# Transposing x0 by batch tile instead of by feature tile, in a six-layer cross network

## The chip, the core and the metric

The kernel runs on one core of a Trainium2 chip, which is trn2. The metric is the device time of one execution in microseconds (us). The time before is the median of six runs.

Engines carry these names in the profile: PE is TensorE's matmul, PEld its weight load, DVE is VectorE, ACT is ScalarE, POOL is GpSimd, SP is SyncE, which here only issues transfers. A name such as L466 is line 466 of the kernel before.

## What is computed

```python
B, F, D, L = 1024, 26, 32, 6
Din = min(F * D, 1024)          # 832
# x0 (1024, 832), ws (6, 832, 832), bs (6, 832), all bfloat16

def reference(x0, ws, bs):
    x = x0
    for l in range(ws.shape[0]):
        x = x0 * (x @ ws[l] + bs[l]) + x
    return x
```

## The kernel before

The kernel keeps x transposed: features on the 128 partitions, the batch of 1,024 along the free dimension. 832 features are six whole tiles of 128 (`KFULL` = 6) and a rest of 64 (`REM`). The rest tile is folded: partitions 0 to 63 hold its first 512 batch rows, partitions 64 to 127 the other 512. So there are `KT` = 7 feature tiles and `BT` = 8 batch tiles of 128 rows (`HBT` = 4 is half of them). The order of all work is written out by hand, engine by engine, with semaphores; no scheduler moves anything.

**The stage in front.** x0 lies in HBM with the batch along the rows. SP loads it into `x0_nat` with three transfers by columns (`x0_dma`, L278): feature tiles 0 and 1, tiles 2 and 3, tiles 4 to 6. GpSimd builds the identity matrix `ident` and then issues the load of the biases, `b_raw` (L348). TensorE first runs `N_WARM` = 24 matmuls on `ident` alone (L364), whose result nobody reads. Then it goes through the feature tiles: tile `kt` takes eight transposes (L397), one for each batch tile, into a PSUM bank of its own in `tr_bank`; the rest tile takes two groups of four (L405, L412). Before feature tile 2 it turns the biases with eight small matmuls into `ps_x` (L371, L378), which waits for `sem_bias`. DVE copies feature tiles 0 to 5 to SBUF, into `x0T`, one copy of 128 x 1024 each (L552); ACT copies `bias_T` (L496) and the rest tile (L504). TensorE begins the layers when all seven copies are done:

```python
eng.wait_ge(sem_cp_v, n_cp_v)
eng.wait_ge(sem_cp_a, n_cp_a)
```

**The layers.** For each layer and each of its seven output tiles (a column group of the weights), TensorE runs seven feature tiles times two batch halves, 14 matmuls with 512 moving columns (L466), into one of two pairs of PSUM banks, `ps_y0` to `ps_y3`. ACT adds the bias on the way to SBUF (L517), DVE multiplies by x0 (L562) and adds x (L576). The last layer's tiles are transposed back and stored.

**The weights.** Layer 0's come in three parts: two blocks of 128 output columns on SP (`w0_dma_block`, L241 to L248) behind x0, and the other 576 columns on ACT's queue (`w0_dma_rest`, L256 to L263), issued once the second x0 transfer has landed. The first matmul of an output tile in layer 0 waits for the part that it needs. Layers 1 to 5 are loaded on SP (L218 to L231), each issued when the layer before it has finished its first item.

Of the kernel before, what the change touches and what calls it, by code (L numbers as in the profile page):

```python
# [5 lines left out]
ACT_F = mybir.ActivationFunctionType  # L6
ALU = mybir.AluOpType
BF16 = mybir.dt.bfloat16
# [3 lines left out]
def bass_standalone__dcn_v2_cross__recsys_kernel(  # L12
# [6 lines left out]
    B, D = x0.shape  # L19
    L = ws.shape[0]  # L20
    P = 128
    NW = 512
    assert B == 2 * NW and D % P == 64 and B % P == 0
    BT = B // P
    HBT = BT // 2
    NCH = 2
    KFULL = D // P
    KT = KFULL + 1
    REM = D - KFULL * P
    RB = KFULL * P  # L30
    NB_COLS = L * KT
# [55 lines left out]
    with ExitStack() as es:  # L87
# [7 lines left out]
        def new_sem(name):  # L95
            return es.enter_context(nc.semaphore(name))

        ident = sb("ident", [P, P], BF16)
# [15 lines left out]
        ps_t1 = psm("ps_t1", [P, 1024], BF16)  # L114
        ps_b = psm("ps_b", [P, NW], FP32)
        ps_x = psm("ps_x", [P, NW], FP32)
        x0_groups = [(0, 2), (2, 4), (4, KT)]
        sem_x0 = [new_sem(f"sem_x0_{i}") for i in range(len(x0_groups))]
        sem_bias = new_sem("sem_bias")
        sem_w = [new_sem(f"sem_w{l}") for l in range(L)]  # L120
        sem_pool = new_sem("sem_pool")
# [20 lines left out]
        ps_t = [ps_t0, ps_t1]  # L142
        xT_bufs = [xT_a, xT_b]

        tr_bank = [
            ps_t0[:, :],
            ps_t1[:, :],
            ps_y0[:, :].bitcast(BF16),
            ps_y1[:, :].bitcast(BF16),
            ps_y2[:, :].bitcast(BF16),  # L150
            ps_y3[:, :].bitcast(BF16),
            ps_b[:, :].bitcast(BF16),
        ]
        assert len(tr_bank) >= KT
        cp_on_act = [False] * KT
        cp_on_act[KT - 1] = True
        cp_wait = []
        n_cp_v = 0
        n_cp_a = 0
        for kt in range(KT):  # L160
            if cp_on_act[kt]:
                n_cp_a += 1
                cp_wait.append((True, n_cp_a))
            else:
                n_cp_v += 1
                cp_wait.append((False, n_cp_v))

        assert NPE == 2
        s_last = (NG - 1) % 2
# [102 lines left out]
        x0_v = x0.rearrange("(bt p) d -> p bt d", p=P)  # L272

        def x0_dma(eng, gi):
            k0, k1 = x0_groups[gi]
            c0 = k0 * P
            c1 = min(k1 * P, D)
            eng.dma_start(x0_nat[:, :, c0:c1], x0_v[:, :, c0:c1]).then_inc(sem_x0[gi], 16)  # L278

        xfin = None  # L280

# [27 lines left out]

        @block.sync  # L310
        def _(eng):
            x0_dma(eng, 0)
            x0_dma(eng, 1)
            x0_dma(eng, 2)
            for jb in range(W0_NBLK):
                w0_dma_block(eng, jb)
            for l in range(1, L):
                eng.wait_ge(sem_mm, mm_items_done_before_layer_start(l))
                w_dma_a(eng, l)
                w_dma_b(eng, l)  # L320
                w_dma_r(eng, l)
            for k in range(len(out_groups)):
                eng.wait_ge(sem_dve, out_groups[k][1] + 1)
                out_transpose(eng, k)
            for (k, c) in pe_pieces:
                if c != 1:
                    continue
                if piece_on_act[(k, c)]:
                    eng.wait_ge(sem_ocpa, piece_wait[(k, c)])
                else:  # L330
                    eng.wait_ge(sem_ocp, piece_wait[(k, c)])
            final_store(eng, 1, sem_out2)
            eng.wait_ge(sem_out2, 16)

        @block.gpsimd
        def _(eng):
            eng.memset(ident[:], 0.0).then_inc(sem_pool, 1)
            eng.wait_ge(sem_pool, 1)
            eng.affine_select(  # L339
                out=ident[:],  # L340
                in_=ident[:],
                compare_op=ALU.not_equal,
                fill=1.0,
                base=0,
                pattern=[[-1, P]],
                channel_multiplier=1,
            ).then_inc(sem_pool, 1)
            eng.dma_start(b_raw[0:L, :], bs[:, :]).then_inc(sem_bias, 16)  # L348
            for k in range(len(out_groups)):
                eng.wait_ge(sem_tro[k], out_transpose_count(k))  # L350
                out_store(eng, k)
            eng.wait_ge(sem_out, 16 * len(out_groups))

        SEM_POOL_WARM = 2
        N_WARM = 24
        ALT_KT_ORDER = False
        BIAS_TR_AFTER_KT = 1
        assert BIAS_TR_AFTER_KT + 1 < KT

        @block.tensor  # L360
        def _(eng):
# [23 lines left out]
                    if last:  # L385
                        mm.then_inc(sem_bt, 1)

            for kt in range(KT):
                pt = tr_bank[kt]
                if kt == BIAS_TR_AFTER_KT + 1:  # L390
                    bias_transposes()
                for gi, (k0, k1) in enumerate(x0_groups):
                    if kt == k0:
                        eng.wait_ge(sem_x0[gi], 16)
                if kt < KFULL:
                    for bt in range(BT):
                        eng.matmul(  # L397
                            pt[:, bt * P : (bt + 1) * P],
                            lhsT=x0_nat[:, bt, kt * P : (kt + 1) * P],
                            rhs=ident[:, :],  # L400
                            is_transpose=True,
                        ).then_inc(sem_tr, 1)
                else:
                    for bt in range(HBT, BT):
                        eng.matmul(  # L405
                            pt[:, (bt - HBT) * P : (bt - HBT + 1) * P],
                            lhsT=x0_nat[:, bt, D - P : D],
                            rhs=ident[:, :],
                            is_transpose=True,
                        ).then_inc(sem_tr, 1)  # L410
                    for bt in range(HBT):
                        eng.matmul(  # L412
                            pt[0:REM, bt * P : (bt + 1) * P],
                            lhsT=x0_nat[:, bt, RB:D],
                            rhs=ident[:, :],
                            is_transpose=True,
                        ).then_inc(sem_tr, 1)
            eng.wait_ge(sem_cp_v, n_cp_v)
            eng.wait_ge(sem_cp_a, n_cp_a)
            for g, (l, j) in enumerate(groups):  # L420
# [69 lines left out]

        @block.scalar
        def _(eng):
            eng.wait_ge(sem_x0[1], 16)
            w0_dma_rest(eng)
            eng.wait_ge(sem_bt, 1)
            eng.activation(bias_T[:, 0:NB_COLS], ps_x[:, 0:NB_COLS], ACT_F.Copy).then_inc(  # L496
                sem_bc, 1
            )
            for kt in range(KT):
                if not cp_on_act[kt]:  # L500
                    continue
                eng.wait_ge(sem_tr, BT * (kt + 1))
                ncol = B if kt < KFULL else NW
                eng.activation(x0T[:, kt, 0:ncol], tr_bank[kt][:, 0:ncol], ACT_F.Copy).then_inc(  # L504
                    sem_cp_a, 1
                )
            eng.wait_ge(sem_bc, 1)
            for f in range(NF - 1):
                l, j, c = items[f]
                g = group_pos[(l, j)]  # L510
                s = g % 2
                slot = f % TB_R
                if f >= TB_R:
                    eng.wait_ge(sem_dve, f - TB_R + 1)
                eng.wait_ge(sem_mm, f + 1)  # L515
                src = ps_y[s][c][:, :] if j < KFULL else ps_y[s][0][:, :]
                eng.activation(  # L517
                    t_buf[:, slot, :],
                    src,
                    ACT_F.Identity,  # L520
                    bias=bias_col(l, j),
                    scale=1.0,
                ).then_inc(sem_act, 1)
            for i, (k, c) in enumerate(pe_pieces):
                if not piece_on_act[(k, c)]:
                    continue
                j = pe_groups[k][0]
                pt = piece_psum(k, c)
                eng.wait_ge(sem_otr, HBT * (i + 1))
                eng.activation(  # L530
                    o_sb[:, c * HBT : (c + 1) * HBT, j * P : (j + 1) * P],
                    pt.rearrange("p (a b) -> p a b", b=P),
                    ACT_F.Copy,
                ).then_inc(sem_ocpa, 1)
            for (k, c) in pe_pieces:
                if c != 0:
                    continue
                if piece_on_act[(k, c)]:
                    eng.wait_ge(sem_ocpa, piece_wait[(k, c)])
                else:  # L540
                    eng.wait_ge(sem_ocp, piece_wait[(k, c)])
            final_store(eng, 0, sem_out3)
            eng.wait_ge(sem_out3, 16)

        @block.vector
        def _(eng):
            for kt in range(KT):
                if cp_on_act[kt]:
                    continue
                eng.wait_ge(sem_tr, BT * (kt + 1))  # L550
                ncol = B if kt < KFULL else NW
                eng.tensor_copy(x0T[:, kt, 0:ncol], tr_bank[kt][:, 0:ncol]).then_inc(sem_cp_v, 1)  # L552

            def emit_mult(f):
                l, j, c = items[f]
# [107 lines left out]
```

## Time and profile before

| | before |
|---|---|
| median of six runs (lowest, highest) | 139.6 us (139.29, 139.91) |
| the profiled execution's own time | 139.72 us |
| its span, first to last instruction | 137.9 us |
| TensorE busy | 127.8 us, 93% of the span |
| DVE, ACT busy | 61.8 us, 52.1 us |
| first matmul of layer 0 (L466) starts | 10.84 us |
| warm-up matmuls (L364) | 24, from 1.52 us, 2.74 us together |
| x0 transfers, issue to landing | 4.2, 5.2 and 6.6 us, issued from 0.74 to 1.87 us |
| bias transfer, issue to landing | 4.8 us, issued at 1.73 us |

Times in rows of the profile are counted from the start of the span. A row of a group gives its line, engine, operation, output and input tiles and shapes, how many there are, and what ended the idle time in front of it. The profiled execution is one execution; the part of its time outside the span, 1.8 us, belongs to no row. Matmuls are pipelined, so that a duration of one is longer than the distance from one to the next.

### The profile page before, as it was taken

To read this page: it belongs to the slowest core of one execution; us is meant where nothing else is said; L and a number is where in the kernel's file an instruction comes from. 1 tells how busy PE (TensorE), PEld (TensorE's weight loads), DVE (VectorE), ACT (ScalarE), POOL (GpSimd) and SP (SyncE) were. 2 spreads that over 40 slices of the span, in tenths; PEclk is the share of its full clock that TensorE was granted. 3 is DMA by queue.
4 is the path that set the end of the run, shared out by engine and by line. 5 is a ranking of instruction groups with operands and counts; after the bars stand their busy time and mean duration, and the time that the engine had idled before them with its cause. 6 is when DMAs were issued, how large, how long until landed. Compare 5 with 4: busy or idle time off the path is not lost.

```text
span 137.9 us, 1868 instructions
## 1 busy us (share of the span) xinstructions
PE 127.8 (93%) x692; PEld 53.9 (39%) x692; DVE 61.8 (45%) x164; ACT 52.1 (38%) x82; POOL 5.8 (4%) x12
## 2 busy tenths in 40 slices
PE   5688999999999999999999999999999999999930
PEld 5463444434344333333443334433444334433410
DVE  0370344554455544554473444463445552554570
ACT  0041444443443353333453334423444333333440
POOL 3000000000000000000000000000000000031520
PEclk9999999999999999999999999999999999999995
DMA  3996670000840001910002900005700000256757
GB/s 79 348 330 177 180 253 0 0 0 0 263 175 0 2 0 16 348 70 5 0 0 66 362 5 0 5 0 158 274 0 0 0 7 0 38 114 152 177 142 214
DMA packets 17016, 13.65 MB, mean 99 GB/s; under 512 B 7242, under 2 KB 16720, under 8 KB 17008
## 3 DMA queue, kind: packets, MB, share of 16 engines
q1 hardware_dynamic: 15136, 11.06, 27.1%
q0 software_dynamic: 400, 1.19, 3.0%
q10 hardware_dynamic: 1472, 1.29, 2.9%
q8 instruction: 5, 0.08, 0.3%
q14 instruction: 3, 0.02, 0.0%
HBM read 10.66 MB, written 1.70 MB: 90 GB/s over the span
## 4 chain that ended last, share of the span: by engine, by line
PE 84%; DMA 8%; DVE 2%; ACT 1%; issue 1%; SPq 1%; POOL 1%; DVEq 0%; ACTq 0%
PE ps_y L466 84%; DMA x_nat<-in_x_dram 5%; DMA o_sb<-xT_b 3%; ACT t_buf L517 1%; DVE x0T L552 1%; SPq L278 1%; DVE u_buf L562 1%; POOL out_dram L305 1%; PE ps_y L397 0%; DVE xT_a L576 0%; DVE xT_b L576 0%; DVEq L561 0%; ACTq L515 0%
## 5 line engine op out<-in xcount | busy, mean ns | idle before, releaser
L517 ACT ACTIVATE t_buf<-ps_y,bias_T 128x512 bf16<-128x512 f32 x77 | 49.1, 683 | 71.7 <-PE ps_y L466 71.7
L562 DVE TENSOR_TENSOR u_buf<-t_buf,x0T 128x512 bf16<-128x512 bf16 x76 | 32.1, 423 | 64.7 <-ACT t_buf L517 64.7
L466 PE MATMUL ps_y<-xT_a,w_sb 128*128 128x512 bf16 (+3 forms) x294 | 60.2, 382 | 0.3 <-DVE xT_a L576 0.3
L466 PE MATMUL ps_y<-xT_b,w_sb 128*128 128x512 bf16 (+3 forms) x196 | 39.9, 381 | 0.0
L466 PEld LDWEIGHTS ps_y<-xT_a,w_sb 128*128 128x128 bf16 (+3 forms) x294 | 23.6, 99 | 36.7 <-issue 13.2
L466 PEld LDWEIGHTS ps_y<-xT_b,w_sb 128*128 128x128 bf16 (+3 forms) x196 | 15.7, 99 | 24.1 <-issue 9.1
L466 PE MATMUL ps_y<-x0T,w_sb 128*128 128x512 bf16 (+3 forms) x98 | 19.9, 381 | 0.7 <-DVE x0T L552 0.7
L576 DVE TENSOR_TENSOR xT_b<-u_buf,xT_a 128x512 bf16<-128x512 bf16 x37 | 15.2, 419 | 0.0
L466 PEld LDWEIGHTS ps_y<-x0T,w_sb 128*128 128x128 bf16 (+3 forms) x98 | 7.8, 98 | 12.7 <-issue 4.1
L576 DVE TENSOR_TENSOR xT_a<-u_buf,xT_b 128x512 bf16<-128x512 bf16 x26 | 10.7, 420 | 0.0
L305 POOL DMA_DIRECT2D out_dram<-o_sb x5 | 4.5, 893 | 127.7 <-DMA o_sb<-xT_b 127.7
L576 DVE TENSOR_TENSOR xT_a<-u_buf,x0T 128x512 bf16<-128x512 bf16 x13 | 5.4, 420 | 0.0
L496 ACT ACT_TABLE_LOAD x1 | 1.3, 1283 | 8.3 <-issue 8.3
L364 PE MATMUL ps_x<-ident 128*128 128x128 bf16 x24 | 2.7, 313 | 1.5 <-POOL ident L339 1.5
L552 DVE COPY x0T<-ps_t 128x1024 bf16<-128x1024 bf16 x2 | 1.3, 688 | 5.6 <-PE ps_t L397 5.6
L364 PEld LDWEIGHTS ps_x<-ident 128*128 128x128 bf16 x24 | 2.5, 147 | 1.5 <-POOL ident L339 1.5
L552 DVE COPY x0T<-ps_y 128x1024 bf16<-128x1024 bf16 x4 | 2.6, 686 | 0.9 <-PE ps_y L397 0.9
L397 PE MATMUL ps_y<-ident,x_nat 128*128 128x128 bf16 x32 | 2.1, 220 | 0.4 <-DMA x_nat<-in_x_dram 0.4
L397 PEld LDWEIGHTS ps_y<-ident,x_nat 128*128 128x128 bf16 x32 | 1.8, 98 | 0.6 <-DMA x_nat<-in_x_dram 0.6
L484 PE MATMUL ps_t<-ident,xT_b 128*128 128x128 bf16 x8 | 0.8, 222 | 1.3 <-DVE xT_b L610 0.9
L397 PE MATMUL ps_t<-ident,x_nat 128*128 128x128 bf16 x16 | 1.1, 220 | 0.7 <-DMA x_nat<-in_x_dram 0.7
L397 PEld LDWEIGHTS ps_t<-ident,x_nat 128*128 128x128 bf16 x16 | 0.9, 98 | 1.0 <-DMA x_nat<-in_x_dram 1.0
(26 smaller groups left out, 10.2 us busy)
## 6 DMA issues: line engine op xcount, KB each, us to landing
w_sb<-in_ws_dram SPq DMA_DIRECT2D x10, 624.0 KB, 4.7
w_sb<-in_ws_dram SPq DMA_DIRECT2D x10, 104.0 KB, 5.2
x_nat<-in_x_dram SPq DMA_DIRECT2D x2, 512.0 KB, 4.7
out_dram<-o_sb POOLq DMA_DIRECT2D x4, 256.0 KB, 3.8
w_sb<-in_ws_dram ACTq DMA_DIRECT2D x1, 864.0 KB, 5.3
x_nat<-in_x_dram SPq DMA_DIRECT2D x1, 640.0 KB, 6.6
w_sb<-in_ws_dram SPq DMA_DIRECT2D x2, 192.0 KB, 5.6
out_dram<-o_sb SPq DMA_DIRECT2D x1, 256.0 KB, 2.3
```

The source lines that it names most:

```text
L278: eng.dma_start(x0_nat[:, :, c0:c1], x0_v[:, :, c0:c1]).then_inc(sem_x0[gi], 16)
L305: eng.dma_start(out[:, c0:c1].rearrange("(bo bi) f -> bi bo f", bi=P), o_sb[:, :, c0:c1],).then_inc(sem_out, 16)
L364: eng.matmul(ps_x[:, 0:P], lhsT=ident[:, :], rhs=ident[:, :], start=True, stop=True)
L397: eng.matmul(pt[:, bt * P : (bt + 1) * P], lhsT=x0_nat[:, bt, kt * P : (kt + 1) * P], rhs=ident[:, :], is_transpose=True,).then_inc(sem_tr, 1)
L466: mm = eng.matmul(o_ap, lhsT=lhsT, rhs=rhs, start=(kt == kt_first), stop=(kt == kt_last), tile_position=(trow, tcol), skip_group_check=(tc ...
L484: eng.matmul(pt[:, bb * P : (bb + 1) * P], lhsT=xf[:, j, bt * P : (bt + 1) * P], rhs=ident[:, :], is_transpose=True,).then_inc(sem_otr, 1)
L496: eng.activation(bias_T[:, 0:NB_COLS], ps_x[:, 0:NB_COLS], ACT_F.Copy).then_inc(sem_bc, 1)
L517: eng.activation(t_buf[:, slot, :], src, ACT_F.Identity, bias=bias_col(l, j), scale=1.0,).then_inc(sem_act, 1)
L552: eng.tensor_copy(x0T[:, kt, 0:ncol], tr_bank[kt][:, 0:ncol]).then_inc(sem_cp_v, 1)
L562: eng.tensor_tensor(u_buf[:, us, :], t_buf[:, slot, :], x0T[rows, tile, cols], ALU.mult,).then_inc(sem_u, 1)
L576: eng.tensor_tensor(xout[rows, tile, cols], u_buf[:, us, :], xin[rows, tile, cols], ALU.add,).then_inc(sem_dve, 1)
```

## The change

x0 is loaded and transposed by batch tile. Four transfers on SP bring two batch tiles each, whole rows of 832 features. TensorE goes through the eight batch tiles; each takes seven transposes into one PSUM bank, and four banks (`ps_y0` to `ps_y3`) are used in turn, so that batch tile 4 waits for the copies of batch tile 0, and so on. Each batch tile is copied with two instructions, one for its six whole feature tiles and one for the rest; even batch tiles go to DVE, odd ones to ACT. The bias transfer moves from GpSimd's queue to SP, behind the four x0 transfers; the bias matmuls stand after batch tile 3, and the ACT copy of `bias_T` between batch tiles 3 and 5. The rest of layer 0's weights moves from ACT's queue to SP, behind the two blocks. The warm-up matmuls go from 24 to 16. The layers and the output are untouched.

```diff
-        x0_groups = [(0, 2), (2, 4), (4, KT)]
+        X0_RG = 2
+        n_x0_dma = BT // X0_RG
...
-        tr_bank = [
-            ps_t0[:, :],
-            ps_t1[:, :],
+        tr_banks = [
             ps_y0[:, :].bitcast(BF16),
             ps_y1[:, :].bitcast(BF16),
             ps_y2[:, :].bitcast(BF16),
             ps_y3[:, :].bitcast(BF16),
-            ps_b[:, :].bitcast(BF16),
         ]
-        cp_on_act = [False] * KT
-        cp_on_act[KT - 1] = True
...
+        def cp_on_act_bt(bt):
+            return bt % 2 == 1
...
+        def emit_x0T_copies(eng, bt, sem):
+            bank = tr_bank_of(bt)
+            cols = slice(bt * P, (bt + 1) * P)
+            eng.wait_ge(sem_tr, KT * (bt + 1))
...
+            cp(
+                x0T[:, 0:KFULL, cols],
+                bank[:, 0 : KFULL * P].rearrange("p (a b) -> p a b", b=P),
+            )
+            c = bt // HBT
+            rows = slice(c * REM, (c + 1) * REM)
+            lcols = slice((bt - c * HBT) * P, (bt - c * HBT + 1) * P)
+            cp(x0T[rows, KFULL, lcols], bank[rows, KFULL * P : (KFULL + 1) * P]).then_inc(sem, 1)
...
         def x0_dma(eng, gi):
-            k0, k1 = x0_groups[gi]
-            c0 = k0 * P
-            c1 = min(k1 * P, D)
-            eng.dma_start(x0_nat[:, :, c0:c1], x0_v[:, :, c0:c1]).then_inc(sem_x0[gi], 16)
+            b0, b1 = gi * X0_RG, (gi + 1) * X0_RG
+            eng.dma_start(x0_nat[:, b0:b1, :], x0_v[:, b0:b1, :]).then_inc(sem_x0[gi], 16)
...
         @block.sync
         def _(eng):
-            x0_dma(eng, 0)
-            x0_dma(eng, 1)
-            x0_dma(eng, 2)
+            for gi in range(n_x0_dma):
+                x0_dma(eng, gi)
+            eng.dma_start(b_raw[0:L, :], bs[:, :]).then_inc(sem_bias, 16)
             for jb in range(W0_NBLK):
                 w0_dma_block(eng, jb)
+            w0_dma_rest(eng)
...
-            eng.dma_start(b_raw[0:L, :], bs[:, :]).then_inc(sem_bias, 16)
...
-        N_WARM = 24
+        N_WARM = 16
-        BIAS_TR_AFTER_KT = 1
+        BIAS_TR_AFTER_BT = 3
...
+            for bt in range(BT):
+                bank = tr_bank_of(bt)
+                if bt == BIAS_TR_AFTER_BT + 1:
+                    bias_transposes()
+                if bt % X0_RG == 0:
+                    eng.wait_ge(sem_x0[bt // X0_RG], 16)
+                if bt >= NBK:
+                    pb = bt - NBK
+                    eng.wait_ge(sem_cp_a if cp_on_act_bt(pb) else sem_cp_v, cp_count(pb))
+                for kt in range(KFULL):
+                    eng.matmul(
+                        bank[:, kt * P : (kt + 1) * P],
+                        lhsT=x0_nat[:, bt, kt * P : (kt + 1) * P],
+                        rhs=ident[:, :],
+                        is_transpose=True,
+                    ).then_inc(sem_tr, 1)
...
         @block.scalar
         def _(eng):
-            eng.wait_ge(sem_x0[1], 16)
-            w0_dma_rest(eng)
...
+            for bt in range(BT):
+                if cp_on_act_bt(bt):
+                    emit_x0T_copies(eng, bt, sem_cp_a)
+                if bt == BIAS_TR_AFTER_BT + 1:
+                    eng.wait_ge(sem_bt, 1)
+                    eng.activation(
+                        bias_T[:, 0:NB_COLS], ps_x[:, 0:NB_COLS], ACT_F.Copy
+                    ).then_inc(sem_bc, 1)
...
         @block.vector
         def _(eng):
-            for kt in range(KT):
-                if cp_on_act[kt]:
-                    continue
-                eng.wait_ge(sem_tr, BT * (kt + 1))
-                ncol = B if kt < KFULL else NW
-                eng.tensor_copy(x0T[:, kt, 0:ncol], tr_bank[kt][:, 0:ncol]).then_inc(sem_cp_v, 1)
+            for bt in range(BT):
+                if not cp_on_act_bt(bt):
+                    emit_x0T_copies(eng, bt, sem_cp_v)
```

More of the change, by code (lines that the diff above doesn't have):

```diff
@@ L116, in bass_standalone__dcn_v2_cross__recsys_kernel @@
         ps_x = psm("ps_x", [P, NW], FP32)
-        x0_groups = [(0, 2), (2, 4), (4, KT)]
-        sem_x0 = [new_sem(f"sem_x0_{i}") for i in range(len(x0_groups))]
+        X0_RG = 2
+        assert BT % X0_RG == 0
+        n_x0_dma = BT // X0_RG
+        sem_x0 = [new_sem(f"sem_x0_{i}") for i in range(n_x0_dma)]
         sem_bias = new_sem("sem_bias")
@@ L151, in bass_standalone__dcn_v2_cross__recsys_kernel, with tr_bank_of, cp_count @@
             ps_y3[:, :].bitcast(BF16),
-            ps_b[:, :].bitcast(BF16),
         ]
-        assert len(tr_bank) >= KT
-        cp_on_act = [False] * KT
-        cp_on_act[KT - 1] = True
-        cp_wait = []
-        n_cp_v = 0
-        n_cp_a = 0
-        for kt in range(KT):
-            if cp_on_act[kt]:
-                n_cp_a += 1
-                cp_wait.append((True, n_cp_a))
-            else:
-                n_cp_v += 1
-                cp_wait.append((False, n_cp_v))
+        NBK = len(tr_banks)
+        def tr_bank_of(bt):
+            return tr_banks[bt % NBK]
+        def cp_on_act_bt(bt):
+            return bt % 2 == 1
+        def cp_count(bt):
+            return bt // 2 + 1
+        n_cp_v = (BT + 1) // 2
+        n_cp_a = BT // 2
+        def emit_x0T_copies(eng, bt, sem):
+            bank = tr_bank_of(bt)
+            cols = slice(bt * P, (bt + 1) * P)
+            eng.wait_ge(sem_tr, KT * (bt + 1))
+            if eng is nc.vector:
+                cp = lambda o, i: eng.tensor_copy(o, i)
+            else:
+                cp = lambda o, i: eng.activation(o, i, ACT_F.Copy)
+            cp(
[6 more added lines that the diff above has]
+            cp(x0T[rows, KFULL, lcols], bank[rows, KFULL * P : (KFULL + 1) * P]).then_inc(sem, 1)
         assert NPE == 2
@@ L354, in bass_standalone__dcn_v2_cross__recsys_kernel @@
         SEM_POOL_WARM = 2
-        N_WARM = 24
+        N_WARM = 16
         ALT_KT_ORDER = False
-        BIAS_TR_AFTER_KT = 1
-        assert BIAS_TR_AFTER_KT + 1 < KT
+        BIAS_TR_AFTER_BT = 3
+        assert BIAS_TR_AFTER_BT + 1 < BT
         @block.tensor
@@ L386, in bias_transposes @@
                         mm.then_inc(sem_bt, 1)
-            for kt in range(KT):
-                pt = tr_bank[kt]
-                if kt == BIAS_TR_AFTER_KT + 1:
+            for bt in range(BT):
+                bank = tr_bank_of(bt)
+                if bt == BIAS_TR_AFTER_BT + 1:
                     bias_transposes()
[L392 to L402, printed above, removed]
-                else:
[L404 to L417, printed above, removed]
@@ new lines, in _ @@
+                if bt < HBT:
+                    eng.matmul(
+                        bank[0:REM, KFULL * P : (KFULL + 1) * P],
+                        lhsT=x0_nat[:, bt, RB:D],
+                        rhs=ident[:, :],
+                        is_transpose=True,
+                    ).then_inc(sem_tr, 1)
+                else:
+                    eng.matmul(
+                        bank[:, KFULL * P : (KFULL + 1) * P],
+                        lhsT=x0_nat[:, bt, D - P : D],
+                        rhs=ident[:, :],
+                        is_transpose=True,
+                    ).then_inc(sem_tr, 1)
@@ L492, in _ @@
         def _(eng):
-            eng.wait_ge(sem_x0[1], 16)
-            w0_dma_rest(eng)
[L495 to L500, printed above, removed]
-                    continue
-                eng.wait_ge(sem_tr, BT * (kt + 1))
-                ncol = B if kt < KFULL else NW
-                eng.activation(x0T[:, kt, 0:ncol], tr_bank[kt][:, 0:ncol], ACT_F.Copy).then_inc(
-                    sem_cp_a, 1
-                )
+            for bt in range(BT):
[6 more added lines that the diff above has]
+                    ).then_inc(sem_bc, 1)
             eng.wait_ge(sem_bc, 1)
@@ L546, in _ @@
         def _(eng):
[L547 to L552, printed above, removed]
+            for bt in range(BT):
+                if not cp_on_act_bt(bt):
+                    emit_x0T_copies(eng, bt, sem_cp_v)
             def emit_mult(f):
```

## The prediction

> **What bounds the kernel now.** I read the chain of waits first, because it says which stage decides the end.
>
> ```profile
> PE 84%; DMA 8%; DVE 2%; ACT 1%; issue 1%; SPq 1%; POOL 1%; DVEq 0%; ACTq 0%
> ...
> 1.87 6.57 DMA x_nat<-in_x_dram
> ...
> 8.48 0.63 PE ps_y L397 x8
> ...
> 9.14 1.30 DVE x0T L552 x2
> ...
> 10.84 99.37 PE ps_y L466 x490
> ```
>
> The first line is the page's share by engine, the others are pieces of the chain in order of time (start, length). From 10.84 us on TensorE runs the layers' matmuls almost without a break to the end, and the change edits nothing there. What it edits lies in front: x0 must arrive, be transposed and be copied to SBUF. So the question is one number: when does the first L466 matmul start? Each microsecond there is one of the span.
>
> Next the timeline of that stage, for ScalarE and TensorE (start, length, group, wait before it).
>
> ```profile
> 1.52 2.74 PE L364 MATMUL ps_x<-ident 128*128 128x128 bf16 x24 [1.52 <-POOL ident L339]
> ...
> 4.96 1.07 PE L397 MATMUL ps_t<-ident,x_nat 128*128 128x128 bf16 x16 [0.70 <-DMA x_nat<-in_x_dram]
> ...
> 6.62 0.42 PE L371 MATMUL ps_x<-ident,b_raw 6*128 6x6 bf16 x7 [0.59 <-DMA b_raw<-in_bs_dram]
> ...
> 6.97 1.07 PE L397 MATMUL ps_y<-ident,x_nat 128*128 128x128 bf16 x16
> ...
> 8.48 1.07 PE L397 MATMUL ps_y<-ident,x_nat 128*128 128x128 bf16 x16 [0.44 <-DMA x_nat<-in_x_dram]
> ...
> 9.58 0.21 ACT L496 ACTIVATE bias_T<-ps_x 128x42 f32<-128x42 f32 x1
> ...
> 10.15 0.60 ACT L504 ACTIVATE x0T<-ps_b 128x512 bf16<-128x512 bf16 x1 [0.36 <-PE ps_b L412]
> ```
>
> The last x0 transfer lets TensorE go at 8.48. The chain then names DVE copies ending at 10.44 and 0.41 us of "issue"; but ScalarE's copy ends at 10.15 + 0.60 = 10.75, and the matmul follows 0.09 us later. So it is ScalarE that releases the matmuls, 2.36 us after the last x0 landing.
>
> Third, the stretches after a weight load of 1,664-byte rows, issued at 13.94 on an empty queue (the last three columns: granted clock, DMA share, GB/s).
>
> ```profile
> 13.94:15.00 1.06, 1.06 (x6) 0.47 (x6) 0.27 (x1) 0.99 (x2) 0.00 (x0) 1.00 0.02 3
> 15.00:16.00 1.00, 1.00 (x6) 0.43 (x5) 0.85 (x3) 0.28 (x1) 0.00 (x0) 1.00 0.86 178
> 16.00:17.00 1.00, 1.00 (x6) 0.31 (x5) 0.07 (x1) 0.03 (x1) 0.00 (x0) 1.00 0.99 349
> 17.00:18.00 1.00, 1.00 (x6) 0.43 (x5) 0.31 (x1) 1.00 (x2) 0.00 (x0) 1.00 1.05 401
> 18.00:19.00 1.00, 1.00 (x6) 0.45 (x5) 1.00 (x4) 0.23 (x1) 0.00 (x0) 1.00 1.04 399
> ```
>
> This is the nearest row to the new x0 loads, whose rows are 1,664 bytes too: 530 KB in the first 3.06 us after the issue, then 400 GB/s. The old x0 load in 512-byte pieces runs at 345 to 350 GB/s in the same view between 4 and 7 us.
>
> **x0's arrival.** x0 is 1,704 KB. By the weight row it is through at 0.74 + 3.06 + (1,704 - 530)/400 = 6.74 us; at the old load's pace it would be about 7.6, where the old one's sum of bytes stands. I take 6.74, because piece size is what the change alters, and keep 7.6. From the last byte to TensorE's start the views give 0.67 (first weight transfer: 639 KB reached at 17.27, landed at 13.94 + 4.0), 0.79 (first x0 group: 524 KB at 4.17, start 4.96) and 0.86 (last x0 group: 7.62 to 8.48). I take 0.86, the same role, and keep 0.67. The last pair of batch tiles is then usable at 7.60, 0.88 earlier than now.
>
> **The moved bias load.** This is the step that gives the gain back. b_raw leaves GpSimd's queue, where it landed at 1.73 + 4.8 = 6.53, and stands on SP behind all four x0 transfers. TensorE waits for it after batch tile 3, and behind that wait are queued the 28 transposes of batch tiles 4 to 7, then every matmul. Tiles 4 and 5 come in the third transfer, whose 1,278 KB are through at 0.74 + 3.06 + 748/400 = 5.67, usable at 6.53; but b_raw's six rows come after the fourth. One row at 400/16 GB/s is 0.07 us, so the wait ends at 7.60 + 0.07 = 7.67 (bounds: 7.41 with the short landing, 8.5 with the old pace). Early x0 tiles thus stop paying: half the transposes start only when everything has landed.
>
> **Transposes after it.** The bias matmuls hold TensorE 6.97 - 6.62 = 0.35. Sixteen transposes take 1.07 and one 0.22, so they start (1.07 - 0.22)/15 = 0.057 apart. Tiles 4 and 5 (14 transposes) are done after 13 x 0.057 + 0.22 = 0.96; the hand-off to a copy is 0.04 (eight transposes end at 5.58, DVE starts at 5.62). ScalarE can start tile 5 at 7.67 + 0.35 + 0.96 + 0.04 = 9.02. Waits for the bank of the tile four before cost nothing: tiles 0 to 3 land by 5.5 (852 KB at 4.61, plus 0.86), their copies end by about 8, and bank reuse by tile 7 comes after 8.8. If that cover failed, each copy late would shift the end by its lateness.
>
> **Copies.** Removed: six DVE copies of 0.69 and one ACT copy of 0.60. Added per batch tile: one copy of 768 columns and one of 128. ScalarE's rows are 207 ns for 42 columns and 597 for 512, so 0.83 ns a column: 0.81 and 0.28 us. Two of ScalarE's copies in a row (L530, 595 ns each) take 1.08 together, so each follow-up gains 0.11. Tiles 5 and 7 are then 0.81 + 0.28 + 0.81 + 0.28 - 0.33 = 1.85 us (2.18 without the overlap). Tile 7's transposes are done at 9.82, before ScalarE is through with tile 5 at about 9.9, so ScalarE is busy without a gap: 9.02 + 1.85 + 0.09 = **10.96** for the first matmul. DVE's share is lighter: 422 ns for 512 and 688 for 1,024 columns give 0.55 + 0.22 a tile; tile 6, transposed by 9.4, is copied by 10.2. The bias copy of 0.21 on ScalarE falls at about 8.2, in a gap.
>
> **What costs nothing.** The ACT table load (1.28) now heads ScalarE's queue without a wait before it, and runs while x0 is on its way; if it came at the first copy instead, tile 1 would be done at about 7.6, still early. The first weight block (229 KB; 267 GB/s from 8 to 9 us) is through 0.86 after x0 and usable at about 8.5, far from 10.96. The rest of layer 0's weights moves from ScalarE's queue to SP, behind eleven other issues, which take 0.4 to 1.7 us each in the rows of before; 1,032 KB at 400 after the second block end near 12, and they are needed two column groups (6.0 us) after the first matmul, at 17. SP is free again well before layer 1's loads.
>
> **Sum.** 10.96 - 10.84 = +0.12 us. The profiled execution took 139.72 (span 137.9 and 1.8 around it); it becomes 139.84. It lies 0.12 above the median of 139.6, so the median comes to **139.7**. With the bounds (arrival 6.74 to 7.6, landing 0.67 to 0.86, no overlap on ScalarE) the first matmul lies between 10.7 and 12.1, so this case spans 139.4 to 140.9, most of it 139.4 to 140.3. A measurement here tells about 0.2% (0.28 us) from no change.
>
> **The clock.** Warm-up matmuls fall from 24 to 16. They start (2.74 - 0.31)/23 = 0.106 apart, the later transposes 0.057: TensorE doubled its pace between 4.26 and 4.96. Sixteen of them last 1.9 us, to 3.4; the transposes of tiles 0 and 1 begin near 4.3. At the end of the run, the stretch from 131.06 to 134.47 with 1.04 us of TensorE work was followed by a granted clock of 0.50; the one from 4.76 to 8.18 with 2.48 us, nearly all transposes, kept full pace.
>
> ```profile
> 4.76:8.18 3.42, 2.48 (x40) 2.10 (x40) 1.84 (x3) 0.00 (x0) 0.00 (x0) 1.00 1.16 340
> 131.06:134.47 3.41, 1.04 (x13) 0.52 (x10) 2.54 (x6) 1.45 (x3) 0.78 (x1) 1.00 0.58 141
> 134.47:137.90 3.43, 0.00 (x0) 0.00 (x0) 0.00 (x0) 0.00 (x0) 0.10 (x1) 0.50 0.74 214
> ```
>
> I read from it that transposes count as work for the clock, and that the changed kernel, with about 1.6 to 2.1 us in such a stretch, keeps it. The Trainium skill ("TensorE: Matmul & The Clock Gate", Part 4) says otherwise: transposes do not count as busy. By that rule the sum would be that of the slower rival below; the row above speaks against it, though eight small bias matmuls in that stretch keep it from being proof.
>
> **Rival, slower: the clock stays at half.** One mechanism, in TensorE, from 3.4 us on: too little work, so that the transposes behind the bias wait run 0.106 apart. It decides if the needed work in a stretch lies above some 1.6 us (the trace brackets it between 1.04 and 2.48). Tile 7 is then transposed at 7.67 + 0.35 + 27 x 0.106 + 0.31 + 0.04 = 11.23, copied 0.98 later, first matmul 12.30: +1.46. If the first layer also runs at half pace for as long as the warm-up did (at most 4.96 - 1.52 = 3.44 us), it loses half of that, 1.7: together +3.2. That is 141.1 to 142.8, and less if the clock rises midway.
>
> **Rival, faster: b_raw is not last.** If its few rows land before the fourth x0 transfer, the pipeline works as drawn. Bias and tiles 4 and 5 start at 6.53; ScalarE starts tile 5 at 6.53 + 1.35 = 7.88 and has done it at about 8.75; tile 7 is usable for TensorE at 7.60, transposed by 8.60; ScalarE ends at 9.73, first matmul 9.82: -1.02, or 138.6. Landing 0.3 before the fourth is worth about a third of it, 139.3. Against it: the x0 groups landed in the order of issue, 1.5 us or more apart. For it: the Trainium skill ("DMA: Bandwidth & Descriptors", on why a DMA increments its semaphore by 16) says a transfer of six rows runs on six engines alone, so it need not wait for the slowest of sixteen; no run here shows it.
>
> **Chances.** Main case 0.50 (of it 0.05 faster, 0.28 within 0.2%, 0.17 slower: its upper bounds reach further than its lower ones). Clock rival 0.30 (0.28 slower, 0.02 within, where the clock rises soon). Early b_raw 0.20 (0.17 faster, 0.03 within). Sums: 0.22, 0.33, 0.45. The range 139.0 to 141.2 takes the main case nearly whole, the half-early b_raw and the mild clock case; about 0.08 lies below and 0.12 above.
>
> **What would show it.** Right: the bias matmuls start within 0.2 us after the fourth x0 landing, at about 7.7, with TensorE idle for over 1 us before them; ScalarE copies tiles 5 and 7 back to back and its end, not DVE's, is followed by the first L466 matmul at about 11.0; transposes 0.057 apart; from there to the end the span keeps its 127.1 us. Wrong: bias matmuls before 7 us (early b_raw), transposes or first matmuls 0.1 or 0.4 apart (clock), a fourth x0 landing after 8 us (no gain from longer rows), or a wait for weights at the first matmul.

## The result and the profile after

| | before | after |
|---|---|---|
| median | 139.99 us (20 runs, 139.29 to 141.12) | 143.28 us (10 runs, 141.49 to 145.44) |
| the profiled execution's own time | 139.72 us | 142.53 us |
| its span | 137.9 us | 140.8 us |
| first matmul of layer 0 starts | 10.84 us | 13.70 us |

The changed kernel is slower: the ratio is 1.017, with a 95% interval of 1.0122 to 1.0217. Ratios and intervals leave out executions more than 1.5% above the fastest of the same kernel, here four of the ten after, while the medians count all; the medians alone would give 1.0235. The forecast of 139.7 us and its range, up to 141.2, both missed. In the profiled execution all of the difference lies in front of the layers: the first layer matmul moved by 2.86 us, the span by 2.9. That execution is 0.75 us below the median of its kernel; no trace of a longer one was kept.

The chain of waits after (start, length, what; the first line is the page's share by engine):

```profile
PE 84%; DMA 7%; DVE 2%; issue 2%; SPq 1%; ACT 1%; POOL 1%; DVEq 0%; ACTq 0%
...
2.77 6.17 DMA b_raw<-in_bs_dram
...
8.98 0.45 PE ps_x L385 x7
...
13.70 99.37 PE ps_y L480 x490
```

Where x0's last transfer stood in the chain, the bias load now stands: 10 KB that land 6.17 us after their issue, at 8.93. The layers' matmuls behind it take the same 99.37 us as before.

The timeline of that stage after:

```profile
1.52 1.89 PE L378 MATMUL ps_x<-ident 128*128 128x128 bf16 x16 [1.52 <-POOL ident L354]
...
3.84 0.82 PE L412 MATMUL ps_y<-ident,x_nat 128*128 128x128 bf16 x6 [0.44 <-DMA x_nat<-in_x_dram]
...
8.98 0.45 PE L385 MATMUL ps_x<-ident,b_raw 6*128 6x6 bf16 x7 [1.07 <-DMA b_raw<-in_bs_dram]
...
9.37 0.82 PE L412 MATMUL ps_y<-ident,x_nat 128*128 128x128 bf16 x6
...
11.08 1.09 ACT L174 ACTIVATE x0T<-ps_y 128x768 bf16<-128x768 bf16 x2 [1.39 <-PE ps_y L426]
...
12.22 0.25 PE L426 MATMUL ps_y<-ident,x_nat 128*128 128x128 bf16 x1
...
12.51 1.09 ACT L174 ACTIVATE x0T<-ps_y 128x768 bf16<-128x768 bf16 x2 [0.34 <-PE ps_y L426]
...
13.70 3.61 PE L480 MATMUL ps_y<-x0T,w_sb 128*128 128x512 bf16 x16 [1.23 <-issue]
```

Six transposes take 0.82 us, of which one is 0.31: they start 0.10 apart, at half pace, where before they started 0.057 apart. That holds for the first batch tile and for those after the bias wait. Only the very last one (0.25 us) is shorter, and the layers then run at full pace (16 matmuls in 3.61 us). ScalarE's copy of tile 7 begins 0.34 us after tile 5's is done: it waits for TensorE. Its end at 13.60 comes 0.10 us before the first layer matmul.

The trace also holds records of the clock that TensorE was granted. The first one of the changed kernel sets in at 12.27 us, when the last transpose was under way; this is what "the clock was raised" means below. The views print 1.00 as the clock for all time before the first record, so that half pace in front of it shows only in the distances between matmuls. Records of one trace lie whole multiples of 3.41 us apart, and the stretches below are counted back from a record in these steps (busy time and matmuls, clock, DMA share, GB/s):

```profile
2.03:5.44 3.41, 2.97 (x26) 1.00 0.97 322
5.44:8.86 3.42, 2.47 (x18) 1.00 1.01 282
8.86:12.27 3.41, 3.29 (x36) 1.00 0.71 192
```

In the experiments below the trace sometimes lacks a layer's first matmul or two. So its start is taken from ScalarE's first copy in layer 0, which begins 3.17 us later at full pace (14.01 - 10.84 before, 16.87 - 13.70 after).

### The profile page after: what moved, and what is told of

Read it like the earlier page. It is cut to its first block, busy times and chain, and to the rows that moved or that the text cites. A ratio compares the mean times of both kernels' runs of the same rounds, so it can differ in the third digit from the quotient of the medians.

```text
span 140.8 us, 1864 instructions
## 1 busy us (share of the span) xinstructions
PE 130.4 (93%) x684; PEld 55.6 (40%) x684; DVE 60.8 (43%) x166; ACT 55.6 (40%) x89; POOL 5.3 (4%) x11
## 4 chain that ended last, share of the span: by engine, by line
PE 84%; DMA 7%; DVE 2%; issue 2%; SPq 1%; ACT 1%; POOL 1%; DVEq 0%; ACTq 0%
PE ps_y L480 82%; DMA b_raw<-in_bs_dram 4%; DMA o_sb<-xT_b 3%; PE ps_y L412 1%; SPq L292 1%; ACT t_buf L525 1%; DVE u_buf L567 1%; POOL out_dram L319 1%; DVE x0T L172 1%; PE ps_x L385 0%; DVE xT_a L581 0%; PE ps_y L426 0%; DVE xT_b L581 0%; DVEq L566 0%; ACTq L523 0%
## 5 line engine op out<-in xcount | busy, mean ns | idle before, releaser
L172 DVE COPY x0T<-ps_y 128x768 bf16<-128x768 bf16 (+1 forms) x8 | 2.9, 387 | 9.7 <-PE ps_y L419 6.3
L174 ACT ACTIVATE x0T<-ps_y 128x768 bf16<-128x768 bf16 (+1 forms) x8 | 4.1, 538 | 6.7 <-PE ps_y L419 5.0
L412 PE MATMUL ps_y<-ident,x_nat 128*128 128x128 bf16 x48 | 6.3, 311 | 0.4 <-DMA x_nat<-in_x_dram 0.4
L412 PEld LDWEIGHTS ps_y<-ident,x_nat 128*128 128x128 bf16 x48 | 4.8, 143 | 1.1 <-DMA x_nat<-in_x_dram 0.7
L378 PE MATMUL ps_x<-ident 128*128 128x128 bf16 x16 | 1.9, 312 | 1.5 <-POOL ident L354 1.5
L378 PEld LDWEIGHTS ps_x<-ident 128*128 128x128 bf16 x16 | 1.6, 146 | 1.5 <-POOL ident L354 1.5
L385 PE MATMUL ps_x<-ident,b_raw 6*128 6x6 bf16 (+1 forms) x7 | 0.5, 172 | 1.1 <-DMA b_raw<-in_bs_dram 1.1
L419 PE MATMUL ps_y<-ident,x_nat 128*64 128x128 bf16 x4 | 1.3, 316 | 0.0
```

What stands on the lines that cost most here:

```text
L172: cp = lambda o, i: eng.tensor_copy(o, i)
L174: cp = lambda o, i: eng.activation(o, i, ACT_F.Copy)
L378: eng.matmul(ps_x[:, 0:P], lhsT=ident[:, :], rhs=ident[:, :], start=True, stop=True)
L412: eng.matmul(bank[:, kt * P : (kt + 1) * P], lhsT=x0_nat[:, bt, kt * P : (kt + 1) * P], rhs=ident[:, :], is_transpose=True,).then_inc(sem_ ...
L419: eng.matmul(bank[0:REM, KFULL * P : (KFULL + 1) * P], lhsT=x0_nat[:, bt, RB:D], rhs=ident[:, :], is_transpose=True,).then_inc(sem_tr, 1)
```

## The experiments

Two theories stood after the result. The clock theory: with eight warm-ups less TensorE stays at half pace through all transposes. The queue theory: the bias load behind x0 on SP holds TensorE up. Four kernels on one chip tell them apart.

**e1_warm24**

```diff
-        N_WARM = 16
+        N_WARM = 24
```

> The changed kernel with 24 warm-up matmuls instead of 16. Clock theory (the eight dropped warm-ups leave TensorE at half pace through all transposes): the transposes go 0.057 apart again, the 28 behind the bias wait take 1.6 us instead of 3.1, ScalarE's copies of tiles 5 and 7 then run back to back, and the first layer matmul moves from 13.70 to about 12.2: 1.4 us or 1.0% below the changed kernel. Queue theory (the bias load behind x0 is the whole loss): the bias matmuls still start near 9.0, transposes stay as they were, time within 0.3 us of the changed kernel.

Measured: 143.70 us, ratio to before 1.0207 (1.0139 to 1.0274). Both theories missed: no gain, though the clock was raised. Its stretches on TensorE (busy time and matmuls, granted clock, DMA share, GB/s):

```profile
4.83:8.25 3.42, 2.09 (x23) 1.00 1.00 292
8.25:11.66 3.41, 2.98 (x33) 0.50 0.77 167
11.66:15.07 3.41, 1.80 (x9) 0.50 0.63 222
15.07:18.49 3.42, 3.42 (x9) 0.50 0.00 0
```

The trace records the clock raised at 4.83, and the transposes of tiles 1 to 3 ran at full pace. Then TensorE sat idle for 1.77 us before the bias matmuls, the clock fell at 8.25, and it came back only at 18.49, some 5 us into the layers: nine of their matmuls fill 3.42 us where seventeen do in the stretch after. The profiled execution took 144.75 us, the longest of the six, but the others show the same: their mean granted clock is 0.958 to 0.982, in the kernel before it is 0.985 to 0.995 (one execution of 171.4 us aside). The wait for the biases undoes the warm-up; e5_filler tests this.

**e2_bias_pool**

```diff
-            eng.dma_start(b_raw[0:L, :], bs[:, :]).then_inc(sem_bias, 16)   # SP
+            eng.dma_start(b_raw[0:L, :], bs[:, :]).then_inc(sem_bias, 16)   # GpSimd, after ident
```

> The changed kernel with the bias load back on GpSimd's queue, 16 warm-ups kept. Queue theory: biases land near 6.5, TensorE goes from tile 3 (7.9) straight to the bias matmuls and tile 4, and the first layer matmul comes at about 12.6 instead of 13.70: 1.1 us less. Clock theory: the wait for the biases is only a part; transposes stay 0.107 apart, so no more than these 1.1 us can come back, and the kernel stays over 1% slower than the one before.

Measured: 142.58 us, ratio 1.011 (1.0044 to 1.0176). The bias matmuls start at 7.86 with no wait, 1.1 us earlier, as the queue theory said. But with 16 warm-ups the transposes stay at half pace (six take 0.82 us here too); in the profiled execution, 143.25 us and so one of the longer ones, the clock was raised only at 16.24, and the first layer began at half pace too, seven matmuls in 3.19 us:

```profile
13.02 3.19 PE L480 MATMUL ps_y<-x0T,w_sb 128*128 128x512 bf16 x7 [1.61 <-issue]
```

This is the clock theory's part: still 1% behind.

**e3_both**

Both edits together.

> Both: 24 warm-ups and the bias load on GpSimd's queue. If clock and queue are the two causes and add: full-pace transposes, bias matmuls near 6.6, tile 7 limited by the landing of the fourth x0 transfer (8.75 in the changed kernel's profile), first layer matmul 10.9 to 11.0, time within 0.3 us of the kernel before; 9.8 and 1 us faster than before if that landing comes at 7.6 as predicted.

Measured: 140.27 us, ratio 1.0015 (0.9983 to 1.0048): no difference from before that can be told. So the two by two table reads: 143.28 with neither edit, 143.70 and 142.58 with one, 140.27 with both; as ratios to before 1.017, 1.0207, 1.011 and 1.0015. The causes do not add; each alone is enough to lose the clock. Timeline of e3_both:

```profile
7.48 0.42 PE L385 MATMUL ps_x<-ident,b_raw 6*128 6x6 bf16 x7
...
7.83 0.51 PE L412 MATMUL ps_y<-ident,x_nat 128*128 128x128 bf16 x6
...
8.82 2.22 ACT L174 ACTIVATE x0T<-ps_y 128x768 bf16<-128x768 bf16 x4 [0.18 <-PE ps_y L426]
```

The clock was raised at 4.55. Six transposes now take 0.51 us, TensorE does not wait for the biases, and ScalarE's four copies for tiles 5 and 7, back to back, are the last thing: 8.82 + 2.22 = 11.04, first layer matmul 14.31 - 3.17 = 11.14.

**e4_before_warm16**

```diff
-        N_WARM = 24
+        N_WARM = 16
```

> The kernel before with 16 warm-up matmuls, nothing else changed. Clock theory: the old order loses full pace too; the 24 transposes behind the last x0 landing take 2.6 us instead of 1.6, first layer matmul at about 11.8 to 12.2 instead of 10.84, time 1.0 to 1.4 us above before. Queue theory: no change, within 0.3 us of before.

Measured: 140.38 us, ratio 1.0024 (0.9991 to 1.0057): inconclusive, between the two theories. The profiled execution (141.09) shows the clock theory's picture: 16 transposes in 1.89 us instead of 1.07, the clock raised at 11.19, first layer matmul 15.41 - 3.17 = 12.24. But the twelve executions spread from 139.66 to 141.09, much as those of the kernel before on that chip do (139.25 to 140.94, the one of 171.4 aside). So in the old order half pace seems to come in some executions only; in the one with a trace it costs 12.24 - 10.84 = 1.40 us.

**e5_filler**: is it the wait for the biases, or the idleness? TensorE waits as long, but works while waiting; with 24 warm-ups.

```diff
                 if bt == BIAS_TR_AFTER_BT + 1:
+                    for i in range(28):
+                        eng.matmul(ps_x[:, 0:P], lhsT=ident[:, :], rhs=ident[:, :], start=True, stop=True)
                     bias_transposes()
```

> The changed kernel with 24 warm-ups, the bias load still behind x0 on SP, and 28 unused matmuls on the identity between batch tile 3 and the wait for the biases, to keep TensorE busy while it waits. Idle theory (the wait costs little by itself; it makes the clock fall at the end of a 3.4 us stretch that holds too little work): the granted clock stays 1.00 from about 5 us on, transposes after the wait 0.057 apart, first layer matmul near 12.3 where e1_warm24 had 13.4, first layer at full pace: about 141.3, some 2.4 us under e1_warm24. Wait theory (the lost time is the wait itself): no better than e1_warm24, 143.7.

Measured: 141.29 us, ratio 1.01 (1.0062 to 1.0139), as the idle theory said: 2.4 us under e1_warm24 by the medians, 1.5 by the ratios, and still above e3_both. Timeline:

```profile
7.59 1.74 PE L406 MATMUL ps_x<-ident 128*128 128x128 bf16 x28
9.26 0.42 PE L385 MATMUL ps_x<-ident,b_raw 6*128 6x6 bf16 x7
...
9.61 0.51 PE L414 MATMUL ps_y<-ident,x_nat 128*128 128x128 bf16 x6
...
10.61 2.21 ACT L174 ACTIVATE x0T<-ps_y 128x768 bf16<-128x768 bf16 x4 [0.68 <-PE ps_y L428]
```

The transposes after the wait run at full pace, the layers too. The end comes later than expected (first layer matmul at 12.92, not 12.3), because the bias matmuls start at 9.26, in e1_warm24 at 8.69. Their row names no wait for the load: the trace has the biases landed at 8.97 (8.64 in e1_warm24), so the later landing makes 0.33 of this delay, and the unused matmuls the other 0.24. One detail differs: the clock was raised at 6.71 here, not at about 5.

**e6_sp_hold**: why does x0 land later than forecast? In e3_both, SP holds the first weight block back until the third x0 transfer has landed.

```diff
...
+            eng.wait_ge(sem_x0[2], 16)
             for jb in range(W0_NBLK):
                 w0_dma_block(eng, jb)
```

> e3_both, with SP waiting for the third x0 transfer before it issues the first weight blocks. If the weight blocks' transfers, issued while x0 is under way, slow x0 down (246 to 310 GB/s between 4.5 and 6 us in the changed kernel's trace, against 400 in the weight loads of later layers): x0 flows at 400 GB/s, fourth landing near 7.6 instead of 8.6, and the first layer matmul waits for the first weight block instead, near 11. If x0's dip has another cause: landings as in e3_both. In both cases the time within 0.4 us of e3_both.

Measured: 140.59 us, ratio 1.0044 (1.0019 to 1.007), a little slower than before. x0 came no sooner: 283 GB/s from 4 to 5 us and 240 from 5 to 6, with no weight transfer issued before 7.93; the slowest x0 landing took 6.7 us, in e3_both 6.3. So the weights behind x0 do not slow it. The first layer matmul (11.51) waited for the held-back weight block.

**e8_half_rows**

```diff
-            eng.dma_start(x0_nat[:, b0:b1, :], x0_v[:, b0:b1, :]).then_inc(sem_x0[gi], 16)
+            for c0, c1 in ((0, D // 2), (D // 2, D)):
+                eng.dma_start(x0_nat[:, b0:b1, c0:c1], x0_v[:, b0:b1, c0:c1]).then_inc(sem_x0[gi], 16)
...
```

> e3_both with each x0 transfer split into two of half rows (832 bytes a piece instead of 1,664). If the long pieces are why x0 comes unevenly (fourth landing 8.55 in e3_both against 7.60 forecast): a steadier flow, 345 GB/s or more between 4 and 6 us, fourth landing at 8.0 or before. If not: landings within 0.3 us of e3_both.

Measured: one execution, 139.84 us. The dip stays (278, 236 and 310 GB/s from 3 to 6 us), and tile 6's transposes start at 8.61, in e3_both at 8.64. In this execution half the length of the pieces changed nothing, so it is not the likely cause.

**e9_weights_first**

```diff
+            w_dma_a(eng, 1)
+            w_dma_b(eng, 1)
+            w_dma_r(eng, 1)
             for gi in range(n_x0_dma):
                 x0_dma(eng, gi)
...
-            for l in range(1, L):
+            for l in range(2, L):
```

> e3_both with layer 1's weights loaded first on SP, ahead of x0; only a look at the flow, the kernel itself must get some 3.5 us slower. If the dip between 4 and 6 us belongs to the start of the execution: the weights, which otherwise flow at 400 GB/s, dip there too, and x0 after them flows at 390 to 400. If it belongs to x0's own pattern (two rows of a partition 128 rows apart): the weights flow at 400 from 4 us on, and x0 dips after them, about 2 us after its first packets.

Measured: one execution, 145.48 us. Stretches of SP (the last three columns: clock, DMA share, GB/s):

```profile
5.00:6.00 1.00, 1.00 1.06 400
6.00:7.00 1.00, 1.00 1.11 240
7.00:8.00 1.00, 1.00 1.05 245
8.00:9.00 1.00, 1.00 1.06 404
```

Weights flow at 400 GB/s up to 6 us, when their 1,384 KB are through; then x0 follows, and the rate falls for 2 us while the engines stay busy (share above 1), so each piece takes longer; then 400 again. In this execution the dip goes with x0, not with the start of the execution. But here it meets x0's first rows, in the other kernels rows between a quarter and three quarters of the way. It also looks different: by the traces' records of single pieces, the median piece of 1,664 bytes takes 112 to 120 ns here from 6 to 8 us, and 69 ns in the stretches around; in the dip of e3_both (205 and 228 GB/s from 4 to 6 us) the median stays at 69 ns and one piece in ten takes more than 100 ns, the longest 1.55 us. So the second theory fits only in part, the two dips may be two effects, and what makes them stays open.

**e7_split**: what is left in e3_both?

```diff
-                if bt == BIAS_TR_AFTER_BT + 1:
-                    bias_transposes()
...
+                    if bt == BT - 1 and kt == KD:  # KD = 4: the rest of tile 7 into ps_t0, copied by ScalarE
+                        bank = ps_t0[:, :]
...
+            bias_transposes()                      # behind the last transposes
...
```

> e3_both, with the bias matmuls behind the last transposes and the last batch tile's copies divided: feature tiles 0 to 3 on DVE, 4 to 6 on ScalarE from a second PSUM bank. If ScalarE's two whole tiles (2.22 us from 8.82) are what is left of the loss in e3_both: first layer matmul at 10.4 to 10.6 instead of 11.14, time 0.6 us under e3_both and 0.2 to 0.4 us under the kernel before. If something else ends last (x0's landing or the first weight block): no gain over e3_both beyond 0.2 us.

Measured: 139.80 us, ratio 0.999 (0.9957 to 1.0023): about 0.5 us under e3_both by the medians, but on another chip and with intervals that overlap; level with before. First layer matmul 14.22 - 3.17 = 11.05: ScalarE was done at 10.79, and now DVE ended last, after waiting for the fourth x0 transfer (tile 6 transposed from 9.12). In this execution x0's landing is the limit, as the second expectation has it, and the first layer matmul gains only 0.09 us on e3_both; the time alone, with a gain between what the two expectations name, does not decide between them.

**e10_before_warm30** and **e11_before_regroup**: what these findings are worth in the old order.

```diff
-        N_WARM = 24
+        N_WARM = 30
# e11_before_regroup, besides:
-        x0_groups = [(0, 2), (2, 4), (4, KT)]
+        x0_groups = [(0, 2), (2, 5), (5, KT)]
+        cp_on_act[3] = True
-            eng.wait_ge(sem_x0[1], 16)     # ScalarE
-            w0_dma_rest(eng)
+            w0_dma_rest(eng)               # SP, behind the two blocks
```

> The kernel before with 30 warm-up matmuls instead of 24, up to the first x0 landing. If the clock is raised at the end of a stretch of 3.4 us with enough work in it, and where the stretches lie changes from execution to execution: fewer executions near 140.8, a median of 139.4 to 139.6. If 24 are enough in every execution: no change, 139.7.

Measured: 139.57 us, ratio 0.9976 (0.9946 to 1.0006). The twelve executions lie between 139.32 and 140.13; of the 23 of before on the same chip ten lay above 140.2. The spread shrank as expected; a gain is not shown by the interval.

> The kernel before with 30 warm-ups, x0's column groups cut as 0-1, 2-4 and 5-6, so that 16 transposes instead of 24 stand behind the last landing, the rest of layer 0's weights moved from ScalarE's queue to SP, and feature tile 3 copied by ScalarE. If what stands behind the last landing sets the first layer matmul: 10.5 instead of 10.84, some 0.3 us under e10_before_warm30. If x0's landing moves later by as much, or DVE's copies end last: no gain.

Measured: 139.37 us, ratio 0.9955 (0.992 to 0.9991): faster than before, by 0.1 to 0.8%. Timeline:

```profile
1.53 3.38 PE L366 MATMUL ps_x<-ident 128*128 128x128 bf16 x30 [1.53 <-POOL ident L341]
4.99 1.73 PE L399 MATMUL ps_t<-ident,x_nat 128*128 128x128 bf16 x16
...
9.72 0.60 ACT L504 ACTIVATE x0T<-ps_b 128x512 bf16<-128x512 bf16 x1 [0.43 <-PE ps_b L414]
...
13.58 1.27 ACT L517 ACTIVATE t_buf<-ps_y,bias_T 128x512 bf16<-128x512 f32 x2 [3.27 <-PE ps_y L468]
```

The warm-ups reach to the first transposes almost without a gap, yet the clock was raised only at 6.41 in this execution, and the first sixteen transposes take 1.73 us instead of 1.07. ScalarE's last copy ends at 10.32, and the first layer matmul is at 13.58 - 3.17 = 10.41, 0.43 earlier than before. Its median is the lowest of all versions tried, but its interval overlaps that of e10_before_warm30; ScalarE's table load heads its queue there (0.74), and the warm-ups and the new groups were not separated further than by e10_before_warm30.

## Why the prediction was wrong, step by step

The forecast first matmul was 10.96, the measured one 13.70. By its own terms:

- **x0's arrival** (7.60 forecast): the fourth transfer landed 6.5 us after its issue at 2.25, at 8.75. The row taken was that of the weight loads, 400 GB/s; x0 began like it (401 GB/s from 3 to 4 us) and ran at 301 to 327 from 4 to 8. The term was too small by 1.15. The upper bound of the forecast (8.5) was nearer. The rate is not all of it: the semaphore of a transfer rises in steps as parts of it land, and the sixteen steps of this one came between 6.87 and 8.76 us, those of the last x0 transfer before between 7.61 and 8.43. So its first part was there well ahead of the forecast, and the wait is for its last part. Loading whole rows brought x0's end no earlier than the old 8.43; why is not known.
- **The moved bias load**: the mechanism was right. It landed 0.18 us after the fourth x0 transfer (0.07 forecast), TensorE was idle for 1.07 us in front of it, and 28 transposes stood behind it. With the arrival, this step is late by 1.31.
- **The clock**: this is the step whose mechanism failed. I wrote that the changed kernel "keeps it". The row this rested on (4.76 to 8.18 us before) shows a clock being kept that was up already, after 24 plain warm-ups; the changed kernel, with 16, first had to raise it, and did not: its first clock record sets in at 12.27. The main case put this at nothing; the half pace costs 0.71 us up to ScalarE's start of tile 5 (1.71 after the transposes' start, 1.00 forecast) and 0.30 more between tiles 5 and 7 (ScalarE's 2.52 us in all, against 2.22 at full pace in e3_both), 1.01 together. The traces of e1_warm24 and e2_bias_pool have half pace into the layers; that the longer executions of the changed kernel (up to 145.44 us) have it too is likely, not shown.
- **ScalarE's copies**: 1.85 forecast, 2.22 at full pace. A copy of 768 columns took 0.81 us, as worked out, but the follow-ups gained nothing like 0.11 each; the bound without overlap (2.18) was nearly right. Too small by 0.37.
- Bias matmuls (0.39, forecast 0.35), DVE's copies (0.80 a tile at most, off the path), weights (not waited for), ACT table load (at 0.73, hidden): as forecast.

Together 1.31 + 0.04 + 0.71 + 0.30 + 0.37 = 2.73, which is 13.70 - 10.96 within rounding. So the late arrival is the largest term that was mis-sized, and the clock the one that was left out. That the clock and the queue make the loss against the kernel before is shown by e3_both: it undoes both, x0 still lands at 8.59 there, and the time is that of before. What the new order could still have gained, 1 us by e3_both's expectation with the fourth landing at 7.6, went to the late arrival and to ScalarE's copies.

The slower rival was the right one, with a chance of 0.30. Its price was set on the forecast arrival: its 12.30 with the 1.31 of the later bias wait gives 13.6, near the 13.70 measured. The forecast did not follow its own rival: it priced it at 141.1 to 142.8 us and left only 0.12 above 141.2.

Its rule does not come out of the traces, though. It was to decide from some 1.6 us of work in a stretch. In e1_warm24 the stretch with 2.09 us of work lost the clock; before, 2.48 us kept it; but 1.84 us in e5_filler and 1.83 us in e6_sp_hold (9.20 to 12.61) kept it as well. The lost stretch held transposes alone and an idle time of 1.77 us; the two others also held plain matmuls of the layers, with idle times of 1.57 and 1.58 us. Which of these decides, no run here separates. For raising the clock the picture is as open: 24 plain matmuls, 2.74 us, did it before, while 2.97 us, about half of it plain matmuls and half transposes (2.03 to 5.44 after), did not, nor did the 2.47 us of transposes in the next stretch. Three stretches, of e2_bias_pool, e5_filler and e4_before_warm16 in turn:

```profile
6.00:9.41 3.41, 3.41 (x34) 1.00 1.03 291
...
10.12:13.53 3.41, 1.84 (x26) 1.00 0.96 292
...
7.77:11.19 3.42, 3.42 (x34) 1.00 1.11 335
```

The first, transposes and the eight small bias matmuls without a break, did not raise the clock. The second kept it. At the end of the third, with transposes alone, it was raised.

The Trainium skill ("TensorE: Matmul & The Clock Gate", Part 4) was set aside in the forecast too lightly. It says that the full clock does not engage for transposes, which do not count as busy in the same way. As it stands this is not what the traces show: in e4_before_warm16 TensorE ran only transposes from 7.77 to 11.19, and the clock rose at the end (so too in e9_weights_first, from 9.45 to 12.86). But transposes did not always raise it where 2.74 us of plain matmuls had, and a forecast by the rule would have come nearer.

The faster rival fell: in the profiled execution the biases landed last, although few rows were asked for. The order is not fixed: in e1_warm24 they landed at 8.64, ahead of the fourth x0 transfer (7.2 us after its issue, at 9.47), but too late to gain anything.

## What to carry to other kernels

Before moving a small load behind a large one on the same queue, ask which engine waits for it and what stands behind that wait; here 10 KB held up half of the transposes and, with TensorE idle, cost the clock as well in e1_warm24. Check TensorE's pace ahead of the main loop, warm-ups and waits included, by the distances between matmuls and not by the clock column alone: two harmless-looking edits (fewer warm-ups, a longer wait) each lost the full clock, and only undoing both brought it back. Do not take a row that shows a clock being kept as proof that it will be raised. An early start of a pipeline is worth what is left behind its last arrival; a smaller last piece with its copies on both engines moved the first layer matmul by 0.09 us in e7_split and, with longer warm-ups, by 0.43 in e11_before_regroup.

## What was not expected of the hardware

In e1_warm24 the granted clock fell after a stretch with a TensorE wait of 1.77 us, and it took 10.2 us, from 8.25 to 18.49, to rise again: the first of these three stretches held 2.98 us of work, the second 1.80 (with a first matmul or two missing from the trace), and the third was full. Raises and falls lie a multiple of 3.41 us apart in each trace (4.83, 8.25 and 18.49 there; 4.76 and 134.47 before), and where these steps lie differs from trace to trace. That one kernel keeps its clock in some executions and loses it in others would follow; the spread of the kernel before, which 30 warm-ups shrank, fits it, but no kernel has two traces here. And x0 read by batch tile loses a quarter to a half of its rate for some 2 us in most kernels here (301 and 313 GB/s after, 205 and 228 in e3_both; e7_split, at 300 GB/s or more throughout, still had its fourth landing at 9.08); read by columns it did not.
